# Recurrent gated attention and a mixture of adapters: from chunk-major to batch-major units of 128 tokens and 8 heads

## The chip, the cores and the metric

The kernel runs on one core of a Trainium2 chip. The core has five engines that work side by side and meet through semaphores: TensorE (matrix products, PE in the profile; its weight loads are PEld), VectorE (DVE), ScalarE (ACT), GpSimd (POOL) and SyncE (SP, which here only issues transfers). Data reach the on-chip memory SBUF by DMA; matrix products land in PSUM, eight banks of 2 KB per partition. Each engine takes its own instructions in a fixed order.

The metric is the device time of one execution in microseconds (us), the median of several runs. Differences of under about 0.3% are within what repeated runs of this kernel show.

## The reference, cut to what matters

Shapes: `q, k, v, alpha` are (4 batches, 8 heads, 768 tokens, 48), all float32; the mixture has 8 experts of rank 16 over 384 = 8 x 48 features.

```python
def _attn_ref(q, k, v, alpha):
    state = zeros((B, H, D, D)); y = zeros_like(q)
    for t in range(S):
        state = alpha[:, :, t, :, None] * state + einsum('bhd,bhe->bhde', k[:, :, t], v[:, :, t])
        y[:, :, t] = einsum('bhd,bhde->bhe', q[:, :, t], state)
    return y

def _moe_ref(x, w_gate, A, B):            # x: the 3072 tokens, 384 features (8 heads side by side)
    logits = x @ w_gate                   # the two largest of 8 experts per token
    w = softmax over these two
    delta = sum over the two experts e of  w[e] * ((x @ A[e]) @ B[e])
    return x + delta
```

## The kernel before, in words

The 768 tokens are cut into 6 chunks of 128 (`C`, `NCH`). The main loop (L389) runs over chunks, and one pass handles all 4 batches and 8 heads of that chunk, 32 (batch, head) rows of 48 floats per token.

- `issue_loads` (L156) issues four transfers of 768 KB on SP's queue: `a_t` (alpha, L158), `q_t` (L160), `k_t` (L162), `v_t` (L164). Each moves 32 rows of 192 bytes per partition. The pool `inpool` (L53) has 2 buffers of each, so chunk c+2 waits until chunk c has been read.
- `prologue` (L167), for the next chunk: logarithm of alpha on ACT (`lg`, L173), three products with a triangular matrix (`cum_ps`, L185), two exponentials of each (`acum`, `ainv`, L189 and L190), 32 products with ones for the decay of the chunk (`rs_ps`, L198) and their exponential (`e_rep`, L203), six products of q and k with the exponentials on POOL (`qg` L208, `kg` L210), and the cast of v on DVE (`vb`, L213).
- `state_update` (L292): 32 products of `kg` and `vb` (`kv_ps`, L302), added on DVE to the decayed state (`state`, L307); the decay itself is a product on DVE at the end of the pass (`S_mid`, L404).
- `transposes` (L216): `qg` and `kg` are turned by TensorE (`q_ps` L222, `k_ps` L231) and copied by DVE (`qtq` L227, `ktq` L236).
- `batch_body` (L239), once for each two batches: eight products give the attention of 128 x 128 tokens for 8 heads (`at_ps`, L248), DVE multiplies them with the causal mask (`at_sb`, L253), and TensorE forms `y_ps` from `at_sb` and `vb` (L261) and from `qtq` and the state (L268), one product per head each. ACT copies the result twice, as float32 (`xt`, L274) and as bfloat16 (`xtb`, L281); TensorE turns the latter (`xt_ps`, L288) and DVE copies it (`xT`, L290). `at_ps` and `y_ps` have one buffer each (L62, L63).
- `moe` (L314) works one chunk late, on all four batches at once: logits (`lps`, L320), the two largest on DVE (L325 to L336), an exponential of the difference (L338), weights (L340 to L350), their transposition and spreading over ranks (L353 to L362), the products with A (`zT_ps`, L367), the weighting (`zw`, L372), the products with B (`dl_ps`, L376), the sum with `xt` on DVE (`o_sb`, L378) and the transfer to memory, issued on POOL's queue (L379). The pool `outp` (L60) has 2 buffers.
- `cum_ps`, `rs_ps`, `kv_ps`, `xt_ps`, `lps`, `wT_ps`, `wr_ps`, `zT_ps` and `dl_ps` all share two PSUM buffers (`ps_m`, tag `misc`, L64).

The order of the instructions on each engine is set by the planner of the language, ahead of the run: it takes the program in the order written, but puts an instruction that waits for nothing ahead of one that waits. Semaphores are put in by it too.

## Time and profile before

| | us |
|---|---|
| median of 3 runs (233.31 to 233.94) | 233.45 |
| span of the profiled execution, first to last instruction | 231.6 |
| busy in it: PE | 133.3 |
| DVE | 119.5 |
| ACT | 75.1 |
| POOL | 71.7 |
| transfers of the inputs on SP's queue (share 59.4% of the span) | 137.6 |

The device time is 1.85 us above the profiled span; what lies around the span is taken as that. No engine is busy for more than 58% of the span, and the transfers are finished long before its end. The page gives the sums; where the time goes is read from the order of events, that is from the timeline, the waits and the busy time by stretch, of which the rows stand below.

### The profile page before, as it was taken

The page shows a single profiled execution, that of the slowest core. Times are in us where ns is not written, and L with a number is a line of the kernel's source. Part 1 is how long each engine was busy: PE and PEld are TensorE (multiplying, and loading weights), DVE is VectorE, ACT ScalarE, POOL GpSimd, SP SyncE. Part 2 cuts the span into 40 slices and gives each one's busy share as a digit, 9 for nine tenths or more (in the row PEclk, how much of TensorE's full clock was granted, in tenths as well). Part 3 has the DMA queues.
Part 4 walks back from the last instruction along what each step waited for, and adds up shares of the span by engine and source line. Part 5 has one row for each costly group of instructions (what it writes and reads, how often), then busy time and mean ns, then how long its engine had stood idle before and what let it go on. Part 6 is the DMA issues. An engine that isn't in the chain of part 4 may idle for free.

```text
span 231.6 us, 3686 instructions
## 1 busy us (share of the span) xinstructions
PE 133.3 (58%) x1511; PEld 88.1 (38%) x1512; DVE 119.5 (52%) x230; ACT 75.1 (32%) x132; POOL 71.7 (31%) x88
## 2 busy tenths in 40 slices
PE   0100337888747267468567569458396665696450
PEld 0000225567635026345246336047263354454230
DVE  5300318376953227946508776128956059565531
ACT  2200880831281066051274045750021710221000
POOL 8500490760000288000485001294001590003011
PEclk9999999999999999955555755555555557555555
DMA  7999999999999926994219940300001100002112
GB/s 142 182 160 128 184 186 188 179 191 170 204 176 186 181 72 107 187 189 63 80 59 159 187 65 0 136 3 1 3 0 68 68 3 0 3 0 97 42 47 89
DMA packets 104096, 24.23 MB, mean 105 GB/s; under 512 B 102800, under 2 KB 102928, under 8 KB 104080
## 3 DMA queue, kind: packets, MB, share of 16 engines
q1 hardware_dynamic: 98688, 18.88, 59.4%
q0 software_dynamic: 1536, 4.72, 5.7%
q10 hardware_dynamic: 3856, 0.41, 1.6%
q8 instruction: 12, 0.20, 0.4%
q14 instruction: 4, 0.03, 0.1%
HBM read 19.28 MB, written 4.72 MB: 104 GB/s over the span
## 4 chain that ended last, share of the span: by engine, by line
issue 32%; PE 23%; POOL 13%; ACT 12%; DVE 9%; DMA 9%; POOLq 0%; SPq 0%; DVEq 0%; ACTq 0%
POOL qg L208 6%; POOL kg L210 5%; DMA q_t<-in_q_dram 5%; PE y_ps L261 4%; DMA out_dram<-o_sb 4%; PE y_ps L268 3%; DVE at_sb L253 3%; ACT acum L189 3%; ACT ainv L190 3%; PE k_ps L231 2%; PE zT_ps L367 2%; PE xt_ps L288 2%; PE q_ps L222 2%; POOL out_dram L379 2%; PE kv_ps L302 2%
## 5 line engine op out<-in xcount | busy, mean ns | idle before, releaser
L379 POOL DMA_DIRECT2D out_dram<-o_sb x24 | 14.4, 603 | 125.6 <-DVE o_sb L378 125.0
L261 PE MATMUL y_ps<-vb,at_sb 128*128 128x48 bf16 x192 | 25.2, 218 | 23.9 <-DVE at_sb L253 18.3
L253 DVE TENSOR_TENSOR at_sb<-at_ps,mask 128x1024 bf16<-128x1024 f32 x24 | 29.3, 1219 | 14.1 <-PE at_ps L248 13.9
L274 ACT ACTIVATE xt<-y_ps 128x384 f32<-128x384 f32 x24 | 11.7, 489 | 76.3 <-PE y_ps L268 76.2
L208 POOL TENSOR_TENSOR qg<-q_t,acum 128x528 bf16<-128x528 f32 (+1 forms) x18 | 22.5, 1266 | 30.2 <-ACT acum L189 24.4
L185 PE MATMUL cum_ps<-lg,lsuf 128*128 128x512 bf16 x17 | 9.6, 594 | 37.9 <-ACT ainv L190 21.0
L210 POOL TENSOR_TENSOR kg<-k_t,ainv 128x528 bf16<-128x528 f32 (+1 forms) x18 | 26.8, 1506 | 0.0
L261 PEld LDWEIGHTS <-at_sb 128*128 128x128 bf16 x192 | 13.9, 113 | 33.3 <-DVE at_sb L253 26.5
L227 DVE COPY qtq<-q_ps 128x1024 bf16<-128x1024 bf16 x12 | 8.3, 690 | 28.6 <-PE q_ps L222 28.5
L268 PE MATMUL y_ps<-S_mid,qtq 48*128 48x48 bf16 x192 | 21.3, 218 | 0.0
L378 DVE TENSOR_TENSOR o_sb<-dl_ps,xt 128x384 f32<-128x384 f32 x24 | 12.6, 552 | 13.9 <-DMA out_dram<-o_sb 12.5
L231 PE MATMUL k_ps<-ident_bf,kg 128*128 128x128 bf16 x96 | 15.2, 307 | 7.7 <-POOL kg L210 7.7
L248 PE MATMUL at_ps<-qtq,ktq 48*128 48x128 bf16 x192 | 16.3, 294 | 1.9 <-DVE at_sb L253 1.8
L222 PE MATMUL q_ps<-ident_bf,qg 128*128 128x128 bf16 x96 | 14.8, 310 | 4.1 <-POOL qg L208 2.9
L189 ACT ACTIVATE acum<-cum_ps 128x512 f32<-128x512 f32 x18 | 11.1, 615 | 18.7 <-PE cum_ps L185 18.7
L307 DVE TENSOR_TENSOR state<-kv_ps,S_mid 48x384 bf16<-48x384 f32 x24 | 13.3, 554 | 6.2 <-PE kv_ps L302 5.6
L288 PE MATMUL xt_ps<-ident_bf,xtb 128*128 128x128 bf16 x96 | 14.8, 312 | 2.7 <-DVE o_sb L378 1.4
L198 PEld LDWEIGHTS <-lg 128*48 128x48 bf16 x192 | 5.2, 128 | 28.0 <-ACT ainv L190 17.1
L203 ACT ACTIVATE e_rep<-rs_ps 48x384 f32<-48x384 f32 x24 | 11.7, 486 | 7.3 <-PE rs_ps L198 7.2
L231 PEld LDWEIGHTS <-kg 128*128 128x128 bf16 x96 | 9.4, 137 | 10.4 <-POOL kg L210 9.8
L268 PEld LDWEIGHTS <-qtq 48*128 48x128 bf16 x192 | 10.1, 101 | 6.0
L288 PEld LDWEIGHTS <-xtb 128*128 128x128 bf16 x96 | 10.7, 146 | 4.3 <-issue 2.5
(68 smaller groups left out, 207.5 us busy)
## 6 DMA issues: line engine op xcount, KB each, us to landing
a_t<-in_alpha_dram SPq DMA_DIRECT2D x6, 768.0 KB, 11.0
q_t<-in_q_dram SPq DMA_DIRECT2D x6, 768.0 KB, 10.4
k_t<-in_k_dram SPq DMA_DIRECT2D x6, 768.0 KB, 10.7
v_t<-in_v_dram SPq DMA_DIRECT2D x6, 768.0 KB, 10.9
out_dram<-o_sb POOLq DMA_DIRECT2D x24, 192.0 KB, 2.2
B_st<-in_moe_B_dram ACTq DMA_DIRECT2D x1, 192.0 KB, 3.5
A_st<-in_moe_A_dram ACTq DMA_DIRECT2D x8, 24.0 KB, 5.1
wg_st<-in_moe_w_gate_dram ACTq DMA_DIRECT2D x8, 1.5 KB, 3.5
```

What stands on the lines that cost most here:

```text
L189: nc.scalar.activation(acum_flat[:, t3 * 512:(t3 + 1) * 512], cum_ps, AF.Exp, scale=-1.0)
L208: nc.gpsimd.tensor_tensor(out=qg[:, h0:h1, 0:D], in0=q_t[:, h0:h1, :], in1=acum[:, h0:h1, :], op=ALU.mult)
L210: nc.gpsimd.tensor_tensor(out=kg[:, h0:h1, 0:D], in0=k_t[:, h0:h1, :], in1=ainv[:, h0:h1, :], op=ALU.mult)
L222: nc.tensor.transpose(q_ps[:, j, :], qg[:, 2 * p:2 * p + 2, :].rearrange("a b s -> a (b s)"), ident_bf[:, :],)
L231: nc.tensor.transpose(k_ps[:, j, :], kg[:, 2 * p:2 * p + 2, :].rearrange("a b s -> a (b s)"), ident_bf[:, :],)
L248: nc.tensor.matmul(at_ps[:, slot, :], ktq[rows, jp, :], qtq[rows, jp, :], start=True, stop=True,)
L253: nc.vector.tensor_tensor(out=at_sb, in0=at_ps, in1=mask8, op=ALU.mult)
L261: nc.tensor.matmul(y_ps[:, tt, j * D:(j + 1) * D], at_sb[:, slot, :], vb[:, bh, :], start=True, stop=False,)
L268: nc.tensor.matmul(y_ps[:, tt, j * D:(j + 1) * D], qtq[rows, jp, :], S_mids[c % 2][rows, p, :], start=False, stop=True,)
L288: nc.tensor.transpose(xt_ps[:, m, :], xtb[:, m, :], ident_bf[:, :])
L307: nc.vector.tensor_tensor(out=S_next[rows, half * 8:(half + 1) * 8, :], in0=kv_ps[rows, :, :], in1=S_mids[c % 2][rows, half * 8:(half + 1) ...
L379: nc.gpsimd.dma_start(out=out[t0:t0 + C, :], in_=o_sb)
```

## The change

The loop order is turned round. Work is cut into 24 units (batch b, chunk c), each of 128 tokens and all 8 heads, and each unit runs attention and then the mixture to its end. Loads come by whole batches: four transfers of 1152 KB each (48 rows of 192 bytes per partition), three buffers deep; batches 0 to 2 are issued at the start and batch 3 when batch 0 has been read. Weights are loaded on SP's queue as well, after batch 0. The prologue works on two chunks of one batch at a time (a "duo") and is written ahead of the units of the duo before. The cast of v moves from DVE to POOL. The state of two heads is kept as one 96-wide block of a 128-row tile, whose off-diagonal quarters are zero; it is carried over in PSUM by a product with the identity, and the decay is applied when it is copied out. The mixture's logits and its products with A are one product of 136 columns; the two largest come from one maximum instruction; the product with B is added to `y` in PSUM, so that no sum on DVE remains. Results go out on SP's queue (`nc.sync`), three buffers deep, in place of POOL's. One activation table is loaded at the start for both functions.

```diff
-    inpool = ctx.enter_context(tc.tile_pool(name="inpool", bufs=2))
-    outp = ctx.enter_context(tc.tile_pool(name="outp", bufs=2))
...
+    loads = ctx.enter_context(tc.tile_pool(name="loads", bufs=3))
     scal = ctx.enter_context(tc.tile_pool(name="scal", bufs=2))
-    qkpool = ctx.enter_context(tc.tile_pool(name="qkpool", bufs=1))
-    trsb = ctx.enter_context(tc.tile_pool(name="trsb", bufs=2))
+    vpool = ctx.enter_context(tc.tile_pool(name="vpool", bufs=3))
+    trsb = ctx.enter_context(tc.tile_pool(name="trsb", bufs=3))
...
+    moep = ctx.enter_context(tc.tile_pool(name="moep", bufs=3))
+    outp = ctx.enter_context(tc.tile_pool(name="outp", bufs=3))
...
+    ps_cum = ctx.enter_context(tc.tile_pool(name="ps_cum", bufs=1, space=PS))
+    ps_tr = ctx.enter_context(tc.tile_pool(name="ps_tr", bufs=1, space=PS))
+    ps_at = ctx.enter_context(tc.tile_pool(name="ps_at", bufs=1, space=PS))
+    ps_y = ctx.enter_context(tc.tile_pool(name="ps_y", bufs=2, space=PS))
+    ps_m = ctx.enter_context(tc.tile_pool(name="ps_m", bufs=2, space=PS))
+
+    nc.scalar.preload_act_table_set("natural_log_exp_and_others")
+
+    def load_batch(b):
+        tiles = []
+        for name, src in (("a_t", alpha), ("k_t", k), ("q_t", q), ("v_t", v)):
+            t = loads.tile([P, H * NCH, 48], F4, name=name, tag=name)
+            nc.sync.dma_start(
+                out=t[:, :, 0:D], in_=src[b].rearrange("h (c j) d -> j (h c) d", j=C))
+            tiles.append(t.rearrange("p (h c) d -> p c h d", h=H)[:, :, :, 0:D])
+        return tiles
+
+    batches = [None] * B
+    batches[0] = load_batch(0)
+
+    W_st = consts.tile([P, NF, NW], F4, name="W_st")
+    for i in range(NF):
+        nc.sync.dma_start(
+            out=W_st[:, i, 0:E * R].rearrange("p (e r) -> p e r", e=E),
+            in_=moe_A[:, i * P:(i + 1) * P, :].rearrange("e f r -> f e r"))
+    nc.sync.dma_start(
+        out=W_st[:, :, E * R:NW], in_=moe_w_gate.rearrange("(i f) e -> f i e", f=P))
+    B_st = consts.tile([P, DM], F4, name="B_st")
+    nc.sync.dma_start(out=B_st, in_=moe_B.rearrange("e r f -> (e r) f"))
+    batches[1] = load_batch(1)
+    batches[2] = load_batch(2)
+
...
+    W = consts.tile([P, NF, NW], F2, name="W")
+    nc.vector.tensor_copy(out=W, in_=W_st)
...
+    def prologue(b, g, ring):
+        a_t, k_t, q_t, v_t = batches[b]
+        cs = slice(g * G, (g + 1) * G)
+        lg, qg, kg = lgs[ring], qgs[ring], kgs[ring]
+        nc.scalar.activation(lg[:, :, :, 0:D], a_t[:, cs], AF.Ln)
+        acum = scal.tile([P, G, H, D], F4, name="acum")
+        ainv = scal.tile([P, G, H, D], F4, name="ainv")
+        dec = scal.tile([P, G, NP], F4, name="dec")
+        for c in range(G):
+            cum = ps_cum.tile([P, 512], F4, name="cum")
+            nc.tensor.matmul(cum[:, 0:DM], tri[:, :], lg[:, c, :, 0:D], start=True, stop=True)
+            for p in range(NP):
+                nc.tensor.matmul(
+                    cum[:, DM + p:DM + p + 1],
+                    lg[:, c, 2 * p:2 * p + 2, :].rearrange("a b s -> a (b s)"), ones[:, :],
+                    start=True, stop=True)
+            nc.scalar.activation(
+                ainv[:, c].rearrange("p h d -> p (h d)"), cum[:, 0:DM], AF.Exp, scale=-1.0)
+            nc.scalar.activation(
+                acum[:, c].rearrange("p h d -> p (h d)"), cum[:, 0:DM], AF.Exp)
+            nc.scalar.activation(dec[:, c, :], cum[:, DM:DM + NP], AF.Exp)
+        for c in range(G):
             nc.gpsimd.tensor_tensor(
+                out=kg[:, c, :, 0:D], in0=k_t[:, g * G + c], in1=ainv[:, c], op=ALU.mult)
             nc.gpsimd.tensor_tensor(
+                out=qg[:, c, :, 0:D], in0=q_t[:, g * G + c], in1=acum[:, c], op=ALU.mult)
+        vb = vpool.tile([P, G, H, D], F2, name="vb")
+        nc.gpsimd.tensor_copy(out=vb, in_=v_t[:, cs])
+        return qg, kg, vb, dec
...
+    def unit(b, c, pro):
+        qg, kg, vb, dec = pro
+        ci = c % G
+        tr = ps_tr.tile([P, 2, NP, P], F2, name="tr")
+        for w, src in enumerate((kg, qg)):
+            for p in range(NP):
+                nc.tensor.transpose(
+                    tr[:, w, p, :],
+                    src[:, ci, 2 * p:2 * p + 2, :].rearrange("a b s -> a (b s)"), ident[:, :])
+        kq = trsb.tile([P, 2, NP, P], F2, name="kq")
+        nc.vector.tensor_copy(out=kq, in_=tr)
+
+        if c + 1 < NCH:
+            kv = ps_m.tile([P, NP, 2, D], F4, name="kv", tag="m")
+            if c > 0:
+                nc.tensor.matmul(
+                    kv.rearrange("p a b d -> p (a b d)"), ident[:, :],
+                    sbd[c % 2].rearrange("p a b d -> p (a b d)"),
+                    start=True, stop=False, skip_group_check=True)
+            for p in range(NP):
+                nc.tensor.matmul(
+                    kv[:, p].rearrange("p b d -> p (b d)"),
+                    kg[:, ci, 2 * p:2 * p + 2, :].rearrange("a b s -> a (b s)"),
+                    vb[:, ci, 2 * p:2 * p + 2, :].rearrange("a b s -> a (b s)"),
+                    start=(c == 0 and p == 0), stop=(p == NP - 1), skip_group_check=True)
+            for hh in range(2):
+                rows = slice(HP * hh, HP * hh + HP)
                 nc.vector.tensor_tensor(
+                    out=sbd[(c + 1) % 2][rows, :, hh, :], in0=kv[rows, :, hh, :],
+                    in1=_bc(dec[rows, ci, :], D), op=ALU.mult)
+
+        at = ps_at.tile([P, 2, NP, P], F4, name="at")
+        for p in range(NP):
+            for hh in range(2):
+                rows = slice(HP * hh, HP * hh + D)
+                nc.tensor.matmul(
+                    at[:, hh, p, :], kq[rows, 0, p, :], kq[rows, 1, p, :],
+                    start=True, stop=True)
+        at_sb = atsb.tile([P, 2, NP, P], F2, name="at_sb")
+        nc.vector.tensor_tensor(
+            out=at_sb.rearrange("p a b t -> p (a b) t"),
+            in0=at.rearrange("p a b t -> p (a b) t"), in1=_bc_mid(mask[:, :], (8,)), op=ALU.mult)
+
+        y = ps_y.tile([P, DM], F4, name="y")
+        first = True
+        if c > 0:
+            for p in range(NP):
+                nc.tensor.matmul(
+                    y[:, p * 2 * D:(p + 1) * 2 * D], kq[:, 1, p, :],
+                    sbd[c % 2][:, p].rearrange("p b d -> p (b d)"),
+                    start=first, stop=False, skip_group_check=True)
+                first = False
+        for p in range(NP):
+            for hh in range(2):
+                h = 2 * p + hh
+                nc.tensor.matmul(
+                    y[:, h * D:(h + 1) * D], at_sb[:, hh, p, :], vb[:, ci, h, :],
+                    start=first, stop=False, skip_group_check=True)
+                first = False
+
+        xb = moep.tile([P, DM], F2, name="xb")
+        nc.scalar.copy(xb, y)
+        xt = ps_m.tile([P, NF, P], F2, name="xt", tag="m")
+        for i in range(NF):
+            nc.tensor.transpose(xt[:, i, :], xb[:, i * P:(i + 1) * P], ident[:, :])
+        xs = moep.tile([P, NF, P], F2, name="xs")
+        nc.vector.tensor_copy(out=xs, in_=xt)
+        z = ps_m.tile([P, NW], F4, name="z", tag="m")
+        for i in range(NF):
+            nc.tensor.matmul(z, xs[:, i, :], W[:, i, :], start=(i == 0), stop=(i == NF - 1))
+        lg_ps = z[:, E * R:NW]
+        mx = moep.tile([P, 8], F4, name="mx")
+        nc.vector.max(mx, lg_ps)
+        df = moep.tile([P, E], F4, name="df")
+        nc.vector.tensor_scalar(df, lg_ps, mx[:, 0:1], None, ALU.subtract)
+        ex = moep.tile([P, E], F4, name="ex")
+        nc.scalar.activation(ex, df, AF.Exp)
+        wu = moep.tile([P, E], F4, name="wu")
+        den = moep.tile([P, 1], F4, name="den")
         nc.vector.scalar_tensor_tensor(
+            out=wu, in0=lg_ps, scalar=mx[:, 1:2], in1=ex, op0=ALU.is_ge, op1=ALU.mult,
+            accum_out=den)
+        rd = moep.tile([P, 1], F4, name="rd")
+        nc.vector.reciprocal(out=rd, in_=den)
+        zw = moep.tile([P, E, R], F2, name="zw")
+        nc.vector.scalar_tensor_tensor(
+            out=zw, in0=z[:, 0:E * R].rearrange("p (e r) -> p e r", e=E), scalar=rd[:, 0:1],
+            in1=_bc(wu[:, :], R), op0=ALU.mult, op1=ALU.mult)
+        zt = ps_m.tile([P, P], F2, name="zt", tag="m")
+        nc.tensor.transpose(zt, zw.rearrange("p e r -> p (e r)"), ident[:, :])
+        zs = moep.tile([P, P], F2, name="zs")
+        nc.vector.tensor_copy(out=zs, in_=zt)
+        nc.tensor.matmul(y, zs[:, :], B_all[:, :], start=False, stop=True, skip_group_check=True)
+        o = outp.tile([P, DM], F4, name="o")
+        nc.scalar.copy(o, y)
+        t0 = b * S + c * C
+        nc.sync.dma_start(out=out[t0:t0 + C, :], in_=o)
+
+    duos = [(b, g) for b in range(B) for g in range(NCH // G)]
+    pros = {0: prologue(0, 0, 0)}
+    for n, (b, g) in enumerate(duos):
+        if n + 1 < len(duos):
+            nb, ng = duos[n + 1]
+            if ng == 0 and nb + 2 < B:
+                batches[nb + 2] = load_batch(nb + 2)
+            pros[n + 1] = prologue(nb, ng, (n + 1) % 2)
+        for c in range(g * G, (g + 1) * G):
+            unit(b, c, pros[n])
```

## Rows read from the trace of the kernel before

**Rows 1.** The page, parts 1 and 2: span, busy times, granted clock, transfer engines' share.

```profile
span 231.6 us, 3686 instructions
PE 133.3 (58%) x1511; PEld 88.1 (38%) x1512; DVE 119.5 (52%) x230; ACT 75.1 (32%) x132; POOL 71.7 (31%) x88
...
PEclk9999999999999999955555755555555557555555
DMA  7999999999999926994219940300001100002112
```

**Rows 2.** Busy time by stretch: start:end, length, busy (instructions) by engine, clock, DMA share, GB/s.

```profile
114.30:147.00 32.70, 22.24 (x253) 14.64 (x253) 19.14 (x37) 15.21 (x24) 10.30 (x10) 0.55 0.60 97
...
128.00:144.00 16.00, 10.57 (x123) 6.92 (x119) 11.68 (x25) 5.54 (x10) 0.00 (x0) 0.61 0.65 84
```

**Rows 3.** Waits: engine and line, what it waited for, total, times, longest.

```profile
DVE o_sb L378 <- DMA out_dram<-o_sb: 12.5, 7, 4.0
...
PE cum_ps L185 <- DVE o_sb L378: 7.4, 3, 4.0
```

**Rows 4.** Timeline: start, length, engine, line, operation, tiles; issues of transfers, ACT's first two.

```profile
0.81 0.44 ACTq L118 DMA_DIRECT2D B_st<-in_moe_B_dram  x1
...
7.80 10.65 ACTq L100 DMA_DIRECT2D A_st<-in_moe_A_dram  x8
...
30.34 4.16 SPq L164 DMA_DIRECT2D v_t<-in_v_dram  x1
...
69.39 4.08 SPq L158 DMA_DIRECT2D a_t<-in_alpha_dram  x1
```

**Rows 5.** Page, parts 3 and 6: packets, MB, share per queue; issue to landing.

```profile
q1 hardware_dynamic: 98688, 18.88, 59.4%
...
q10 hardware_dynamic: 3856, 0.41, 1.6%
...
a_t<-in_alpha_dram SPq DMA_DIRECT2D x6, 768.0 KB, 11.0
...
out_dram<-o_sb POOLq DMA_DIRECT2D x24, 192.0 KB, 2.2
```

**Rows 6.** The chain that ended last, in order of time: start, length, what; its first step.

```profile
1.29 10.98 DMA q_t<-in_q_dram
```

**Rows 7.** Groups by line and form: shapes, count; busy, mean ns; idle before them, releaser.

```profile
L253 DVE TENSOR_TENSOR at_sb<-at_ps,mask 128x1024 bf16<-128x1024 f32 x24 | 29.3, 1219 | 14.1 <-PE at_ps L248 13.9
...
L208 POOL TENSOR_TENSOR qg<-q_t,acum 128x528 bf16<-128x528 f32 x12 | 15.5, 1299 | 30.2 <-ACT acum L189 24.4 <-issue 5.8
...
L378 DVE TENSOR_TENSOR o_sb<-dl_ps,xt 128x384 f32<-128x384 f32 x24 | 12.6, 552 | 13.9 <-DMA out_dram<-o_sb 12.5 <-PE dl_ps L376 1.2
L274 ACT ACTIVATE xt<-y_ps 128x384 f32<-128x384 f32 x24 | 11.7, 489 | 76.3 <-PE y_ps L268 76.2
...
L290 DVE COPY xT<-xt_ps 128x512 bf16<-128x512 bf16 x24 | 10.1, 422 | 3.9 <-PE xt_ps L288 3.8
...
L227 DVE COPY qtq<-q_ps 128x1024 bf16<-128x1024 bf16 x12 | 8.3, 690 | 28.6 <-PE q_ps L222 28.5
...
L173 ACT ACT_TABLE_LOAD x6 | 7.7, 1283 | 1.4 <-PEq L422 1.3
...
L325 DVE TENSOR_REDUCE m<-lps 128x4 f32<-128x32 f32 x6 | 1.1, 184 | 0.4 <-PE lps L320 0.4
```

**Rows 8.** Timeline of TensorE: four bursts of matmuls, start, length, count at the end.

```profile
37.11 1.04 PE L222 MATMUL q_ps<-ident_bf,qg 128*128 128x128 bf16 x8 [1.20 <-DVE qtq L227]
...
45.45 0.61 PE L248 MATMUL at_ps<-qtq,ktq 48*128 48x128 bf16 x8
...
72.29 1.89 PE L367 MATMUL zT_ps<-xT,A_arr 128*128 128x128 bf16 x16
...
203.90 1.89 PE L367 MATMUL zT_ps<-xT,A_arr 128*128 128x128 bf16 x16
```

**Rows 9.** Timeline, the last two results issued on POOL's queue.

```profile
226.97 1.19 POOL L379 DMA_DIRECT2D out_dram<-o_sb  x2 [2.05 <-DVE o_sb L378]
```

More of the change, by code (lines that the diff above doesn't have):

```diff
@@ L63 @@
[L63 to L70 removed]
+    moep = ctx.enter_context(tc.tile_pool(name="moep", bufs=3))
+    outp = ctx.enter_context(tc.tile_pool(name="outp", bufs=3))
+    PS = bass.MemoryType.PSUM
@@ new lines @@
+    ones = consts.tile([P, 1], F2, name="ones")
+    nc.gpsimd.memset(ones, 1.0)
+    lgs, qgs, kgs = [], [], []
+    for i in range(2):
+        for lst, nm in ((lgs, "lg"), (qgs, "qg"), (kgs, "kg")):
+            t = consts.tile([P, G, H, HP], F2, name=f"{nm}{i}")
+            nc.gpsimd.memset(t[:, :, :, D:HP], 0.0)
+            lst.append(t)
+    ident = consts.tile([P, P], F2, name="ident")
+    make_identity(nc, ident)
+    mask = consts.tile([P, P], F4, name="mask")
+    nc.gpsimd.memset(mask, 1.0)
@@ L89 @@
-    nc.gpsimd.affine_select(
-        out=Rmat, in_=Rmat, compare_op=ALU.is_ge, fill=0.0, base=(R - 1),
-        pattern=[[-1, E * R]], channel_multiplier=R,
-    )
-    A_st = consts.tile([P, NM, E, R], F4, name="A_st")
-    nc.gpsimd.memset(A_st, 0.0)
-    for m in range(NM):
-        for which in range(2):
-            base = 64 * which
-            h = 2 * m + which
-            nc.scalar.dma_start(
-                out=A_st[base:base + D, m, :, :],
-                in_=moe_A[:, h * D:(h + 1) * D, :].rearrange("e f r -> f e r"),
-            )
@@ L104 @@
-    A_arr = consts.tile([P, NM, E * R], F2, name="A_arr")
-    nc.vector.tensor_copy(out=A_arr, in_=A_st.rearrange("p m e r -> p m (e r)"))
-    wg_st = consts.tile([P, NM, E], F4, name="wg_st")
-    nc.gpsimd.memset(wg_st, 0.0)
-    for m in range(NM):
-        for which in range(2):
-            base = 64 * which
-            h = 2 * m + which
-            nc.scalar.dma_start(out=wg_st[base:base + D, m, :], in_=moe_w_gate[h * D:(h + 1) * D, :])
-    wg_arr = consts.tile([P, NM, E], F2, name="wg_arr")
@@ L115 @@
-    nc.vector.tensor_copy(out=wg_arr, in_=wg_st)
-    B_st = consts.tile([P, DM], F4, name="B_st")
-    nc.scalar.dma_start(out=B_st, in_=moe_B.rearrange("e r f -> (e r) f"))
+        out=mask, in_=mask, compare_op=ALU.is_ge, fill=0.0, base=0,
+        pattern=[[1, P]], channel_multiplier=-1,
+    )
+    sbd = []
+    for i in range(2):
+        t = consts.tile([P, NP, 2, D], F2, name=f"sbd{i}")
+        nc.vector.memset(t, 0.0)
+        sbd.append(t)
+    W = consts.tile([P, NF, NW], F2, name="W")
@@ L119 @@
+    nc.vector.tensor_copy(out=W, in_=W_st)
     B_all = consts.tile([P, DM], F2, name="B_all")
     nc.vector.tensor_copy(out=B_all, in_=B_st)
-    st_tiles = []
-    for i in range(2):
-        st = persist.tile([P, NPAIR, D], F2, name=f"state{i}")
-        nc.vector.memset(st, 0.0)
-        st_tiles.append(st)
-    qg_tiles, kg_tiles = [], []
-    for i in range(2):
-        qg = qkpool.tile([P, BH, 64], F2, name=f"qg{i}")
-        nc.gpsimd.memset(qg[:, :, D:64], 0.0)
-        kg = qkpool.tile([P, BH, 64], F2, name=f"kg{i}")
-        nc.gpsimd.memset(kg[:, :, D:64], 0.0)
-        qg_tiles.append(qg)
-        kg_tiles.append(kg)
@@ L381 @@
-    loads = [None] * NCH
-    loads[0] = issue_loads(0)
-    if NCH > 1:
-        loads[1] = issue_loads(1)
-    vbs = [None] * NCH
-    vbs[0] = prologue(0, loads[0])
-    xt_lists = [None] * NCH
-    for c in range(NCH):
-        xt_list = [None] * B
-        xt_lists[c] = xt_list
-        state_update(c, vbs[c])
-        qtq0, ktq0 = transposes(c, 0)
-        qtq1, ktq1 = transposes(c, 1)
-        if c >= 1:
-            moe(c - 1, xt_lists[c - 1])
-        if c + 1 < NCH:
-            if c + 2 < NCH:
-                loads[c + 2] = issue_loads(c + 2)
-            vbs[c + 1] = prologue(c + 1, loads[c + 1])
-        batch_body(c, 0, qtq0, ktq0, vbs[c], xt_list)
-        batch_body(c, 1, qtq1, ktq1, vbs[c], xt_list)
-        if c + 1 < NCH:
-            nc.vector.tensor_tensor(
-                out=S_mids[(c + 1) % 2], in0=st_tiles[(c + 1) % 2],
-                in1=e_reps[(c + 1) % 2], op=ALU.mult)
```

281 lines of the change are left out of this document (15 added, 266 removed).

## The prediction

> **What bounds the kernel now.** I read the page first. In the 231.6 us of the profiled execution no engine is busy for more than 58%, and the transfer engines are full for the first 19 of 40 slices and then mostly idle [rows 1]. So neither a single engine nor memory bounds the whole; the limits change on the way. Up to about 75 us the loads are the limit: SP issues nine 768 KB loads one behind the other between 30.34 and 69.39 us, 4.34 us each [rows 4], which is 0.181 MB/us. From then on the period of a chunk is the limit. One period, 114.3 to 147.0, lasts 32.7 us for four (batch, chunk) units, 8.2 us a unit, with PE busy for 22.2, DVE 19.1, ACT 15.2 and POOL 10.3 us [rows 2]: each waits for another for a third of the time or more. The waits show where: `cum_ps` of the next chunk stands behind `o_sb`, which shares its two PSUM buffers, and `o_sb` stands for 12.5 us in all behind results that have not landed, with two buffers [rows 3]. Then ACT, POOL and the transposes run one after another, and the copy of `q_ps` on DVE has 28.6 us of idle time before it [rows 7]. In the second half of a period, 128 to 144, four units of attention and of the mixture pass in 16.0 us with DVE busy for 11.68 us, 73% [rows 2]; that is the best mixing this trace shows.
>
> The row of the clock reads 9 for the first 18 slices and mostly 5 after [rows 1], yet the same 16 products of `zT_ps` take 1.89 us at 72.29 and at 203.90 [rows 8]. So I price products by their durations, which are alike on both sides: 16 of 128 columns take 0.85 us more than 8, 0.83 ns a column, which is the level of 1.2 GHz.
>
> **The change, part by part.** I sum each engine's work for one of the 24 units, find a pace, and then look for what holds units up.
>
> DVE. A product or sum that reads PSUM costs 1219 ns for 1024 elements and 552 for 384, so 152 ns plus 1.04 per element; a bfloat16 copy costs 690 for 1024 and 422 for 512, so 154 plus 0.52 per element; a tiny operation 184 [rows 7]. A unit has one copy of 1024 (`kq`, 0.69), two decays of 192 elements in five units of six (2 x 0.35 x 5/6 = 0.59), one mask (1.22), copies of 384 and 128 (0.36 and 0.22), one weighting of 128 (0.29) and four tiny ones (0.74): 4.1 us. The sums `o_sb`, the casts of v and the state's second addition go; 24 units make 98 us where DVE had 119.5 [rows 1].
>
> PE. Columns streamed per unit: 1024 (transposes of `kg`, `qg`), 576 (identity product and `kv`, on average), 320 and 384 (`y`), 384 (`xt`), 408 (`z`), 128, 384 (the product with B) and 384 (`cum`): 3992 x 0.83 ns = 3.3 us. The eight `at` products go in pairs, 0.61 us where eight full ones took 1.04 [rows 8], so 0.4 us, and four one-column products about 0.1: 3.8 us.
>
> ACT. Four passes over 384 elements at 0.489 [rows 7], half a logarithm of 768 and two tiny ones at most as much each: under 3.4 us. Twelve reloads of its table go, of which the row shows six, 7.7 us [rows 7]; the 3.4 us is under the pace found below, so this brings nothing by itself. POOL. Two products of 384 at 1299/528 ns per element are 1.9 us; the cast of v has no row on POOL, and I bound it by nothing and by that price, 0 to 0.94: at most 2.8 us, hidden as the prologue runs a duo ahead.
>
> Pace. DVE at 100% gives 4.1 us a unit, DVE at the 73% of the best stretch 4.1/0.73 = 5.6. There is more to hand over per unit than before (ten changes of engine from `y` to `o`), but `y` has two buffers, `kq` three, `cum` a bank of its own. I take 5.0, somewhat nearer to the row that was measured.
>
> Loads. The bytes and the 192-byte rows stay: q1 had 98,688 packets for 18.88 MB [rows 5], and 16 x 6144 is 98,304. A load of 1152 KB takes 1.5 x 4.34 = 6.5 us. The first two loads landed at 12.27 us [rows 6]; the rest of batch 0, 3.15 MB, takes 17.4 us more: 29.7. The weights, now on the same queue, took 1.6% of the span on their own [rows 5], 3.7 us: 33.4. Eight loads of batches 1 and 2 land by 33.4 + 52.1 = 85.5, batch 3 by 111.5.
>
> Results. This is the step on which the forecast turns. Results move from POOL's queue to SP's. SP's issue of a load lasts as long as the transfer itself, 4.16 and 4.08 us [rows 4], and a load lands 11.0 us after it was begun [rows 5]: SP is held until the queue takes the load, about 11.0 - 4.3 = 6.7 us ahead of landing. Loads 1 and 2 wait for nothing, so the planner sets them ahead of every result; the trace shows it do so, where the load of B, written last, goes out at 0.81 and those of A, which wait for a memset, at 7.80 [rows 4]. So SP is free of batch 2 at 85.5 - 6.7 = 78.8. The load of alpha for batch 3 waits only for logarithms, done long before, and I set it ahead of the first result too: 85.3. The first result then lands at 85.3 + 6.7 + 1.1 (0.2 MB) = 93.1. The other three loads of batch 3 hold SP for another 19.5 us, to 104.8, and I set the next results behind them: 112.6.
>
> Who waits: the copy `o` on ACT has three buffers. With the weights there at 33.4 and about 4 us from `z` to `o`, unit 0 is done at 37.5, units 1 and 2 at 42.5 and 47.5. Unit 3 would be at 52.5 and waits for 93.1, unit 4 for 112.6; behind `o` stand on ACT the copies `xb` and the exponentials of later units, and so PE and DVE. Before, results had POOL's queue to themselves and landed in 2.2 us with loads in flight [rows 5].
>
> The Trainium skill, "DMA: Bandwidth & Descriptors", section "Queues, rings and completion order", speaks against this edit: each issuing engine has one ring on every transfer engine, consumed in order, while different rings take turns. The rows of SP agree, and the time by that rule is the forecast; without it, the first rival.
>
> The sum. Unit 4 at 112.6, unit 5, held in the second `y` buffer, 1.5 us later, 18 more units at 5.0: 204.1. From the last two issues to the end 231.6 - 226.97 = 4.6 [rows 9]: a span of 208.7. The device time lies 1.85 above the span (233.45 - 231.6): **210.5 us**. With a pace of 4.1 it is 194, with 5.6 it is 221.
>
> **The rivals.** First, the results are not held up: SP reaches them between loads, or the loads leave SP early. For it: a queue with room takes a transfer at once, the load of B in 0.44 us at 0.81 [rows 4]. Against it: the nine equal issues. Then 37.5 + 23 x 5.0 + 4.6 + 1.85 = **159 us**, 138 to 173 with the ends of the pace.
>
> Second, slower: the mixture at the end of each unit makes the units go one by one. Each engine keeps its order, so while a unit goes from `y` to `o` (about 5.5 us by the prices above: `y` 0.8, `xb` 0.5, `xt` 0.5, `xs` 0.4, `z` 0.5, the small steps 1.0, `zw` 0.3, `zt` and `zs` 0.5, product 0.5, `o` 0.5), DVE puts the next unit's mask and copy (1.9) in between: 7.4 us a unit, **254 us**. It decides from a pace of (233.45 - 114.1 - 6.45)/18 = 6.3. Against it: before, with one buffer of `y` and of `at`, four units of attention and mixture passed in 16.0 us [rows 2].
>
> Third, TensorE gets the higher clock. The row of the clock has two slices of 7 in its second half, so the upper level is granted now and then [rows 1]. At 2.4 GHz PE's 3.8 us become about 2 and DVE alone sets the pace, 4.1 to 4.6: **194 to 203 us**. The Trainium skill, "TensorE: Matmul & The Clock Gate", section "What's actually happening", says that activity releases the gate; the row shows it fall back each time.
>
> Fourth, the change does not do what its first words say: denser rows would have to shorten the loads, and I give that nothing, since the packets stay 192 bytes. If they did by a third, SP is free 35 us earlier and the time is 175.
>
> **How the numbers follow.** Forecast (results trapped, pace 4.7 to 5.6) 0.58; trapped with a faster pace 0.07; results free 0.18; shorter loads 0.04; one by one 0.13. Faster by over 0.3% is 0.85, within 0.3% (what a measurement of this kernel can tell from no change) 0.02, slower 0.13. The range leaves out most of the one-by-one case and the fast end of the free one: 158 to 226.
>
> **What would show it.** In the profile after: SP's issues of the loads back to back for 6.5 us each and the first issue of `out_dram` after 75 us; a wait of ACT's `o` for `out_dram` of 30 to 60 us in all, before 115 us; PE nearly idle from about 55 to 93; after 115 us a result every 5 us. A first result out before 50 us proves the trap wrong; a result every 6.3 us or more makes the kernel slower; DVE's busy time far from 98 us proves the prices wrong.

## The result, and the profile of the changed kernel

The changed kernel takes 201.53 us (median of four runs, 200.92 to 201.69) where the kernel before took 233.47 beside it: a ratio of 0.8627, with a 95% interval of 0.861 to 0.8644. The forecast was 210.5, with a range of 158 to 226. The sign and the mechanism (results trapped behind loads) came true, but the closeness of 9 us is partly luck: two terms of the sum were wrong by 33 and 26 us, in opposite directions, as the sections below show. A time is the median of all runs of a kernel; in one kernel below (the weights' loads moved) three of four runs fell into a slower state of the chip, its trace among them, and there the fourth run's time stands.

The page of the changed kernel, parts 1 and 2, to be read beside [rows 1]:

```profile
span 199.9 us, 2870 instructions
...
PE 109.8 (55%) x1064; PEld 77.1 (39%) x1064; DVE 98.1 (49%) x284; ACT 59.0 (30%) x157; POOL 59.7 (30%) x77
...
PEclk9999999968555555555555555555855555555555
DMA  5899989799989999899902101110011011101111
```

DVE is busy for 98.1 us, forecast 98, and the transfer engines are again full for half of the span and idle after it. The device time lies 1.6 us above the span.

SP's timeline, the end of the loads (start, length, operation, count), answers to [rows 4]; below it ScalarE's copies `o`, each of which ends one unit:

```profile
61.54 4.74 SPq L77 DMA_DIRECT2D v_t<-in_v_dram  x1
66.38 6.30 SPq L255 DMA_DIRECT2D out_dram<-o  x3
72.89 0.70 SPq L77 DMA_DIRECT2D a_t<-in_alpha_dram  x1
74.55 4.86 SPq L255 DMA_DIRECT2D out_dram<-o  x1
79.63 0.70 SPq L77 DMA_DIRECT2D k_t<-in_k_dram  x1
...
91.08 106.22 SPq L255 DMA_DIRECT2D out_dram<-o  x20
```

```profile
48.73 0.48 ACT L253 COPY o<-y 128x384 f32<-128x384 f32 x1 [1.83 <-PE y L251]
...
74.04 1.01 ACT L253 COPY o<-y 128x384 f32<-128x384 f32 x2 [13.99 <-DMA out_dram<-o]
...
81.41 0.48 ACT L253 COPY o<-y 128x384 f32<-128x384 f32 x1 [2.90 <-PE y L251]
...
130.85 0.48 ACT L253 COPY o<-y 128x384 f32<-128x384 f32 x1 [2.41 <-PE y L251]
...
170.92 0.48 ACT L253 COPY o<-y 128x384 f32<-128x384 f32 x1 [2.47 <-PE y L251]
```

The trap is plain: three results are done by 49 us and leave only at 66.38, straight after the last load of batch 2; units 3 and 4 come together at 74.04, after ScalarE has stood 13.99 us for a result to land. Then two further results come, then a second stall, taken up in the section on more buffers. From unit 12 (130.85) to unit 18 (170.92), the same place in the next batch, six units take 40.07 us, 6.7 us each. That is the steady pace. The last three units, with no prologue left to run beside them, need 4.6 us or less each.

### The profile page after: what moved, and what is told of

It reads as the page before. It is cut to its first block, busy times and chain, and to the rows that moved or that the text cites. A ratio compares the mean times of both kernels' runs of the same rounds, so it can differ in the third digit from the quotient of the medians.

```text
span 199.9 us, 2870 instructions
## 1 busy us (share of the span) xinstructions
PE 109.8 (55%) x1064; PEld 77.1 (39%) x1064; DVE 98.1 (49%) x284; ACT 59.0 (30%) x157; POOL 59.7 (30%) x77
## 5 line engine op out<-in xcount | busy, mean ns | idle before, releaser
L151 POOL TENSOR_TENSOR kg<-k_t,ainv 128x384 bf16<-128x384 f32 x24 | 23.8, 997 | 76.8 <-ACT ainv L145 38.4
L169 DVE COPY kq<-tr 128x1024 bf16<-128x1024 bf16 x24 | 16.5, 687 | 45.2 <-PE tr L165 30.6
L198 DVE TENSOR_TENSOR at_sb<-at,mask 128x1024 bf16<-128x1024 f32 x24 | 29.4, 1224 | 5.0 <-PE at L194 3.0
L194 PE MATMUL at<-kq 48*128 48x128 bf16 x192 | 15.7, 299 | 22.5 <-DVE kq L169 17.8
L153 POOL TENSOR_TENSOR qg<-q_t,acum 128x384 bf16<-128x384 f32 x24 | 23.6, 997 | 4.4 <-ACT acum L147 2.8
L139 PE MATMUL cum<-lg,tri 128*128 128x384 bf16 x24 | 11.8, 490 | 19.6 <-ACT lg L133 9.9
L165 PE MATMUL tr<-ident,kg 128*128 128x128 bf16 x96 | 15.2, 300 | 11.0 <-POOL kg L151 10.2
L156 POOL CAST vb<-v_t 128x768 bf16<-128x768 f32 x12 | 9.8, 827 | 33.7 <-PE y L214 16.4
L194 PEld LDWEIGHTS <-kq 48*128 48x128 bf16 x192 | 8.6, 123 | 28.7 <-DVE kq L169 22.3
L165 PE MATMUL tr<-ident,qg 128*128 128x128 bf16 x96 | 16.3, 303 | 5.4 <-POOL qg L153 5.4
L186 DVE TENSOR_TENSOR sbd<-kv,dec 64x192 bf16<-64x192 f32 x40 | 14.2, 355 | 7.4 <-PE kv L179 5.6
L206 PE MATMUL y<-sbd,kq 128*128 128x96 bf16 x80 | 10.9, 271 | 12.6 <-ACT o L253 12.6
L214 PE MATMUL y<-vb,at_sb 128*128 128x48 bf16 x192 | 14.3, 218 | 0.5 <-ACT o L253 0.5
```

Of the source, the lines that this page charges most:

```text
L139: nc.tensor.matmul(cum[:, 0:DM], tri[:, :], lg[:, c, :, 0:D], start=True, stop=True)
L151: nc.gpsimd.tensor_tensor(out=kg[:, c, :, 0:D], in0=k_t[:, g * G + c], in1=ainv[:, c], op=ALU.mult)
L153: nc.gpsimd.tensor_tensor(out=qg[:, c, :, 0:D], in0=q_t[:, g * G + c], in1=acum[:, c], op=ALU.mult)
L165: nc.tensor.transpose(tr[:, w, p, :], src[:, ci, 2 * p:2 * p + 2, :].rearrange("a b s -> a (b s)"), ident[:, :])
L169: nc.vector.tensor_copy(out=kq, in_=tr)
L186: nc.vector.tensor_tensor(out=sbd[(c + 1) % 2][rows, :, hh, :], in0=kv[rows, :, hh, :], in1=_bc(dec[rows, ci, :], D), op=ALU.mult)
```

## Experiments

Two theories carried the study. First, the results trapped behind loads on SP's queue cost some 20 us. Second, the pace of 6 to 7 us where 5.0 was forecast, with VectorE 60% busy, comes from the planned order and from prologues that wait for buffers. A third question was why loads left SP sooner than forecast. The planner orders each engine's instructions anew when a buffer or a queue changes, so an edit moves more than itself; where the order stayed the same, it is said.

### Results on another queue

```diff
-        nc.sync.dma_start(out=out[t0:t0 + C, :], in_=o)
+        nc.scalar.dma_start(out=out[t0:t0 + C, :], in_=o)
```

> One edit: the 24 result transfers are set by ScalarE's queue instead of SP's, so they no longer stand behind the loads. The order of the instructions on the other engines is planned anew by the planner. Theory (results trapped behind loads): in the changed kernel unit 3's `o` came at 74.0 us, 25.3 us after unit 2's at 48.7, where a pace of 6 us would have given 6; that is 19 us. Units 7 and 8 came 16.3 us after unit 6 instead of 12; that is 4 more. The time falls by 15 to 24 us, to 177 to 187, the 14.0 us wait of ScalarE's `o` on a result's transfer is gone, and results come about every 6 us from 49 us on. Rival (the stretch is held by the loads of the data themselves, not by the results): the time stays within 2 us of 201.5, and `o` of unit 3 still comes after 70 us.

176.57 us, ratio to the kernel before 0.7558 (0.7539 to 0.7577), just under the range that the theory gave. ScalarE's copies `o` of units 2 and 3:

```profile
50.48 0.48 ACT L253 COPY o<-y 128x384 f32<-128x384 f32 x1 [2.19 <-PE y L251]
...
55.37 0.48 ACT L253 COPY o<-y 128x384 f32<-128x384 f32 x1 [0.17 <-PE y L251]
```

Busy time over one steady batch, `o` of unit 12 to `o` of unit 18 (length, then busy time and instructions of PE, PEld, DVE, ACT, POOL, then granted clock, DMA share, GB/s):

```profile
110.19:145.81 35.62, 21.96 (x269) 16.06 (x267) 23.71 (x71) 13.55 (x39) 13.98 (x15) 0.74 0.10 35
```

Unit 3 comes at 55.37 instead of 74.04, 18.7 us earlier, and it waits for TensorE, not for a result. The last `o` is 24.9 us earlier (171.58 against 196.46). So 18.7 of the 25 us are the hold-up of unit 3; the other 6 come later, where this kernel runs six units in 35.6 us instead of 40.1. Its order is new and its granted clock 0.74 there against 0.54 (the row of the changed kernel stands in the section on one batch). The clock alone does not do it: the four runs of the changed kernel had mean granted clocks of 0.62, 0.90, 0.62 and 0.61 and took 201.57, 201.69, 200.92 and 201.5 us. The order or the queue is left, and no run separates these two.

### More buffers for results, on the old queue

```diff
-    outp = ctx.enter_context(tc.tile_pool(name="outp", bufs=3))
+    outp = ctx.enter_context(tc.tile_pool(name="outp", bufs=8))
```

> One edit: 8 buffers for `o` instead of 3; the results still stand behind the loads on SP's queue. Theory (the trap works through ScalarE's wait for a free `o`): units 3 to 7 no longer wait, the first results still land after 70 us, and the time falls by 12 to 24 us, to 177 to 190, about as with results on another queue. Rival (what is late is the queue itself, so that only moving the results helps): within 2 us of 201.5.

184.42 us, ratio 0.7891 (0.7858 to 0.7924). The results still leave SP late (the first at 66.79), but units 3 to 7 are done at 54.1 to 81.0, since nothing on ScalarE waits for them. Only then, with the next units held:

```profile
80.98 0.48 ACT L253 COPY o<-y 128x384 f32<-128x384 f32 x1 [2.41 <-PE y L251]
...
97.37 0.87 ACT L253 COPY o<-y 128x384 f32<-128x384 f32 x2
```

So the trap works as the prediction had it, through ScalarE's wait for a free `o`; a later stall of 16.4 us stays. A stall of the same length stands between units 6 and 7 of the changed kernel (87.92 to 104.21, 16.3 us) and, at 16.3 us again, in the two runs with other loads below, so it does not hang on how long loads take. With three sets of prologue buffers it is 13.7 us (86.88 to 100.62). With two sets it is not there at all when results go on ScalarE's queue or one batch alone is loaded: 7.7 and 7.4 us at the same place. So two sets alone don't make it. The timeline of the changed kernel shows what it consists of:

```profile
87.92 0.48 ACT L253 COPY o<-y 128x384 f32<-128x384 f32 x1 [2.47 <-PE y L251]
...
94.86 0.52 PE L251 MATMUL y<-B_all,zs 128*128 128x384 bf16 x1
...
98.14 0.21 ACT L235 ACTIVATE ex<-df 128x8 f32<-128x8 f32 x1 [5.19 <-DVE df L233]
...
103.84 0.48 ACT L147 ACTIVATE acum<-cum 128x384 f32<-128x384 f32 x1
104.21 0.87 ACT L253 COPY o<-y 128x384 f32<-128x384 f32 x2
```

The last product of unit 7 ends at 95.38, but ScalarE's order has the exponential of unit 8 (98.14) and seven prologue steps (100.98 to 104.32) ahead of its copy `o`. The stall lies in the planned order; why the planner chose it in these programs stays open.

### Rows that are not adjacent

```diff
-        t = loads.tile([P, H * NCH, 48], F4, name=name, tag=name)
+        t = loads.tile([P, H * NCH, 52], F4, name=name, tag=name)
```

> One edit: a row of 48 floats takes 52 places in the SBUF tile of a load, so that rows are not adjacent; bytes, instructions and their order on each engine are those of the changed kernel. Theory (adjacent rows travel as packets of 768 bytes, and that is why a load took 5.1 us of SP's queue instead of the 6.5 forecast): the packets are 192 bytes again, about 98,300 of them, a load holds SP some 6.3 to 6.6 us, v of batch 2 is set by about 78 us instead of 66, the first results go 10 to 13 us later, and the time is 209 to 218. Rival (the rate comes from fewer other transfers at the time, not from the packets): loads take 5.1 us as now and the time stays within 2 us of 201.5.

209.16 us, ratio 0.8951 (0.893 to 0.8972). The order of every engine is that of the changed kernel, so this is the cleanest run. First the queue of SP of the changed kernel, from part 3 of its page (packets, MB, share of 16 engines), then the same row and two issues of this run:

```profile
q1 hardware_dynamic: 31952, 24.00, 51.5%
```

```profile
q1 hardware_dynamic: 31952, 24.00, 56.0%
...
67.29 5.57 SPq L77 DMA_DIRECT2D v_t<-in_v_dram  x1
72.97 7.05 SPq L255 DMA_DIRECT2D out_dram<-o  x3
```

The number of packets is the same (here and below, the time of a packet is the mean over the trace's records of q1's packets of that size): the theory's mechanism fell, adjacent rows are not what makes the packets large. Yet the time rose, because a packet of 768 bytes took 64.5 ns instead of 56.1. Batch 2 left SP 6.6 us later (72.86 against 66.28), unit 3 came 7.5 us later and the whole kernel ended 7.6 us later: the time is in the theory's range, but for another reason. So the length of the loads passes through the trap to the end nearly one for one.

### Six transfers for one tensor

```diff
-            nc.sync.dma_start(
-                out=t[:, :, 0:D], in_=src[b].rearrange("h (c j) d -> j (h c) d", j=C))
+            for c in range(NCH):
+                nc.sync.dma_start(
+                    out=t.rearrange("p (h c) d -> p c h d", h=H)[:, c],
+                    in_=src[b, :, c * C:(c + 1) * C, :].rearrange("h j d -> j h d"))
```

> One edit: a tensor of a batch is loaded by six transfers, one for each chunk of 128 tokens, into the same places of the same tile; a partition's rows of 48 floats in one transfer are then 8, one head apart, not 48 of equal distance. Bytes are the same; the order is planned anew. In the kernel before, whose loads went chunk by chunk, a packet was 192 bytes and took 22.3 ns; in the changed kernel it is 768 bytes and takes 56.1 ns, and with rows not adjacent in SBUF still 768 bytes, at 64.5 ns. Theory (the whole-batch form of the source, rows of equal distance over all chunks, is what puts four rows into a packet): about 98,300 packets of 192 bytes at 20 to 23 ns, a tensor of a batch holds SP 6.2 to 7 us, and the time is 208 to 222. Rival (the packets come from the tile's dense layout or from batch-major order itself): packets stay at 768 bytes and the time is within 5 us of 201.5.

202.24 us, ratio 0.8672 (0.8634 to 0.8711). The queue's row in part 3, and the end of the loads on SP:

```profile
q1 hardware_dynamic: 106960, 24.01, 55.6%
...
67.59 5.43 SPq L78 DMA_DIRECT2D v_t<-in_v_dram  x6
73.51 1.33 SPq L257 DMA_DIRECT2D out_dram<-o  x3
```

Here each theory got half. The packets are 192 bytes again (98,304 of them), so the whole-batch form of the source is what put four rows into one. But they took 15.5 ns each, not the 22.3 of the kernel before. Rows of one transfer lie apart in SBUF here as in the run with 52 places, so these two compare: four packets of 192 bytes, 61.8 ns, against one of 768, 64.5 ns. Between these two runs, which differ in the number of transfers too, the size of the packet is worth nothing. The adjacent rows are worth about a tenth of the time that a load holds SP (5.6 us a tensor here, 5.1 in the changed kernel, means of the long issues of batches 0 to 2). And the end did not follow this time: SP's queue took the first three results in 1.33 us instead of 6.30, so unit 3 came only 3.2 us later than in the changed kernel. The Trainium skill, "DMA: Bandwidth & Descriptors", section "Specifications", wants 512 bytes or more in a transfer for the full rate. The two packets above don't test that, since a row of a load is 192 bytes in both. But packets of 1536 bytes, one row each, took 69.5 ns for the results of the changed kernel and 65.0 ns for the load of B (on ScalarE's queue) in the kernel before, 22 to 24 bytes per ns where the loads of these runs moved 12 to 14: the trace agrees with the page.

### The kernel before, its loads in four parts

```diff
-        nc.sync.dma_start(out=a_t, in_=chunk_view(alpha, c))
+        for b in range(B):
+            nc.sync.dma_start(
+                out=a_t[:, b * H:(b + 1) * H, :], in_=chunk_view(alpha, c)[:, b * H:(b + 1) * H, :])
...
```

> This one edits the kernel before: each of its loads (one tensor, one chunk, 32 rows of 192 bytes to a partition) is set as four transfers of 8 rows, one for each batch, into the same places; bytes and the order on VectorE, ScalarE and GpSimd are the same. In the changed kernel, packets of 192 bytes in transfers of 8 rows took 15.5 ns, against 22.3 ns in the kernel before. Theory (what made the kernel before's packets slow is the long transfer of 32 rows, whatever the packet's size): packets stay at 192 bytes and take 15 to 18 ns, a tensor of a chunk holds SP 3.2 to 3.8 us instead of 4.1, and the time falls to 212 to 229. Rival (it is what ran beside the loads or the tile's place): 21 to 23 ns a packet and a time within 3 us of 233.4.

230.98 us, ratio 0.9892 (0.987 to 0.9913); the queue's row, beside [rows 5]:

```profile
q1 hardware_dynamic: 99840, 18.88, 56.2%
```

A packet took 20.8 ns (22.3 before), a tensor of a chunk still held SP about 4.2 us. The theory fell: shorter transfers alone don't give the 15.5 ns. These transfers have the form of those above (8 rows, one head apart) with the rows adjacent in SBUF, and go slower, so the gain from adjacent rows is shown for the changed kernel's packets of 768 bytes alone. Why the same 192 bytes went faster in the batch-major kernel stays open.

### Three buffers for a prologue

```diff
-    scal = ctx.enter_context(tc.tile_pool(name="scal", bufs=2))
+    scal = ctx.enter_context(tc.tile_pool(name="scal", bufs=3))
...
-    for i in range(2):
+    for i in range(3):
         for lst, nm in ((lgs, "lg"), (qgs, "qg"), (kgs, "kg")):
...
-            pros[n + 1] = prologue(nb, ng, (n + 1) % 2)
+            pros[n + 1] = prologue(nb, ng, (n + 1) % 3)
```

> One edit: three buffers instead of two for what a prologue writes (lg, qg, kg, and acum, ainv, dec); the order is planned anew. Theory (the pace of 6.0 us after 112 us, where VectorE is only 60% busy, is set by prologues that wait for buffers: GpSimd's kg waits 16 us in all for kv of an earlier unit there): the pace falls to 5.0 to 5.5 us and the time to 183 to 194, with the stall of 49 to 74 us as before. Rival (the pace is the unit's own chain through TensorE, VectorE and ScalarE in the planned order): pace 5.8 to 6.2, time within 4 us of 201.5.

189.40 us, ratio 0.8101 (0.8073 to 0.8129). Waits from 112 to 168 us (total, times, longest), first of the changed kernel, then of this run, last of the run with results on ScalarE's queue, which has two sets:

```profile
POOL kg L151 <- PE kv L179: 16.3, 4, 5.7
...
POOL vb L156 <- PE kv L179: 10.9, 2, 5.6
...
PE tr L165 <- POOL kg L151: 5.0, 7, 1.3
```

```profile
POOL vb L156 <- PE kv L179: 4.8, 1, 4.8
...
POOL kg L151 <- PE kv L179: 4.7, 3, 3.7
...
PE tr L165 <- POOL kg L151: 1.9, 1, 1.9
```

```profile
PE tr L165 <- POOL kg L151: 4.4, 4, 1.7
...
POOL kg L151 <- PE kv L179: 1.4, 1, 1.4
```

Six units now take 34.8 us (5.8 each), and the hold-up up to 73.67 is as before. The theory holds in direction and time; the pace missed its 5.0 to 5.5. The order is new as well, and the run with results on ScalarE's queue came to 35.6 us a batch with two sets, though TensorE stood nearly as long for `kg` there. So this run alone does not show how much is the buffers'.

### One batch loaded

```diff
-    batches[1] = load_batch(1)
-    batches[2] = load_batch(2)
+    batches[1] = batches[2] = batches[3] = batches[0]
...
-            if ng == 0 and nb + 2 < B:
-                batches[nb + 2] = load_batch(nb + 2)
```

> Part of the computation is left out: only batch 0 is loaded, and all 24 units work on its tiles, so that 18 of the 24 units wait for no load and no result stands behind one for long. The planned order is new. Theory (the pace of 6.0 us from 112 us on, and the 5.9 us at which the kernel with results on ScalarE's queue ran from 37 to 172 us, is the planned order's and its two buffers', whatever the loads do): the first `o` at 34 to 37 us, then 5.7 to 6.1 us a unit, time 168 to 180. Rival (loads in flight slow the units, or their data comes late): 5.0 us a unit or less, time 150 to 160.

187.73 us, ratio 0.8039 (0.802 to 0.8059): above the range that the theory gave, and far from its rival. Busy time over one steady batch, in the columns given above, first of the changed kernel, then of this run:

```profile
130.85:170.92 40.07, 26.55 (x269) 18.86 (x266) 24.07 (x71) 13.71 (x39) 13.97 (x15) 0.54 0.09 30
```

```profile
116.67:156.87 40.20, 26.89 (x269) 19.08 (x266) 24.05 (x71) 13.71 (x39) 13.97 (x15) 0.50 0.09 30
```

With no load in flight and none to wait for, a batch takes 40.20 us where it took 40.07. The steady pace has nothing to do with the loads. It is also 6.7 us a unit and not the 6.0 that I had read off a stretch that held the fast last units, which is why the run came out above its range.

### Both edits, and the weights' loads moved

> Two edits together: results on ScalarE's queue, and three buffers for what a prologue writes. Alone they gave 176.6 and 189.4 of 201.5 us. Theory (two separate causes, the trap and the pace): the gains nearly add, 25 and 12, less some 3 since with the third buffer the trap is shorter: first `o` at 37 us, a pace of 5.2 to 5.4 us, time 160 to 170. Rival (the same time counted twice, or the loads of batch 3 become the bound): 173 to 178.

The diffs of the first and of the sixth section together: **169.52 us**, ratio 0.7264 (0.7223 to 0.7305), the fastest of all. The gains of 25.0 and 12.1 alone make 32.0 together; the pace, 5.7 us, missed the 5.2 to 5.4 expected. One steady batch:

```profile
106.12:140.07 33.95, 22.29 (x264) 17.08 (x261) 23.97 (x71) 11.25 (x34) 13.01 (x14) 0.72 0.10 36
```

VectorE is at 71% there, against 60% in the changed kernel.

```diff
-        nc.sync.dma_start(
+        nc.scalar.dma_start(
             out=W_st[:, i, 0:E * R].rearrange("p (e r) -> p e r", e=E),
...
```

> The two edits of the kernel before this one, and the loads of W_st and B_st set by ScalarE's queue at the start instead of behind batch 0 on SP's. Theory (loads of a queue go one after the other on SP, 7.8 us of it for the weights, so batches 1 to 3 are set 7 to 8 us earlier; batch 0 itself is shared with the weights and ends about as now): the first `o` comes at 34 to 37 us, the time is 0 to 6 us under the run without this edit. Rival (the weights delay batch 0 by as much as they are off the queue and nothing after depends on a load): no change, within 1 us.

With the weights on ScalarE's queue too, it is 169.87 us, of one run, between the 168.43 and 170.27 us of two runs without this edit: no change seen, as the rival said. SP set batch 1 at 20.04 instead of 26.49 us, and the first `o` came no earlier.

### The order of the instructions

The hand order, in the slot of unit `u` (`n` is `u + 1`, `m` is `u + 2`), drawn together here into two lines without the conditions for the last units, and the switch of each run, with a remark behind it:

```diff
+        m_xt(u); s_kq(m); m_z(u); s_yi(n); s_y(n); m_ex(u); s_kv(m); s_at(m); s_sbd(m)
+        m_zw(u); m_zt(u); s_atsb(m); m_out(u); s_tr_pe(m + 1); pro(u + 5)
...
-    with _tile.TileContext(nc) as tc:
+    with _tile.TileContext(nc, linearize=True) as tc:                    # by hand
+    with _tile.TileContext(nc) as tc:                                    # hand order, planned
+    with _tile.TileContext(nc, schedule_with_timeline_sim=True) as tc:   # other priorities
```

> The changed kernel with its order written out by hand instead of planned: in the slot of unit u each engine gets the MoE steps of u, y of u+1, and the transposes, state and masked product of u+2, with the prologue of u+5; VectorE gets kq and the state update where it would wait for TensorE and ScalarE. Results go by ScalarE's queue, three buffers for what a prologue writes, as in the run with those two edits (169.5 us). Theory (the pace is the planned order's, with VectorE 60% busy at 6.0 us a unit; the floor is VectorE's 4.1): the first `o` at 36 to 40 us, 4.8 to 5.3 us a unit, time 150 to 166. Rival (TensorE at the lower clock or the units' own chain sets the pace): 5.5 us a unit or more, 168 to 180.

573.61 us, ratio 2.457 (2.4523 to 2.4617). This run says nothing of the theory: the switch that kept my order also put all engines' instructions one after the other. The next two let the planner overlap them again.

> The program of the hand-ordered run, but with its order on each engine planned by the planner again: the run before had put the instructions of all engines one after the other (573.6 us, the sum and not an overlap), so it told nothing of the pace. What is left of the hand order is the sequence in which the steps reach the planner: MoE of u, y of u+1, state and masked product of u+2, prologue of u+5. Theory (the pace is the planned order's): 4.8 to 5.3 us a unit, time 152 to 166. Rival (TensorE at the lower clock or the unit's own chain): 5.4 us or more, 167 to 178.

175.04 us, ratio 0.748 (0.745 to 0.7509). A batch takes 32.9 us from unit 12 on (5.5 a unit), a little under the 33.95 of the run above, but a stall of 12.6 us between units 3 and 4 (54.97 to 67.54), where TensorE is given the transposes and scores (`at`) of three later units first, costs more than that. The 4.8 to 5.3 expected did not come; pace and time are the rival's.

> The program of the run with results on ScalarE's queue and three prologue buffers (169.5 us, 5.5 us a unit), instruction for instruction, with SP's order unchanged; only the planner's way of setting priorities is its other one, and so the order on TensorE, VectorE, ScalarE and GpSimd. Theory (order sets the pace): the pace moves by 0.2 us a unit or more, and the time leaves 165 to 174 in one direction or the other. Rival (buffers, TensorE's clock or the unit's own chain set it, whatever the order): 5.3 to 5.7 us a unit, 166 to 173.

187.97 us, ratio 0.8035 (0.8013 to 0.8057): 18.5 us from the same instructions in another order. ScalarE's timeline, and one steady batch:

```profile
39.10 0.48 ACT L253 COPY o<-y 128x384 f32<-128x384 f32 x1 [1.44 <-PE y L251]
...
56.96 0.37 ACTq L255 DMA_DIRECT2D out_dram<-o  x1
57.38 0.48 ACT L220 CAST xb<-y 128x384 bf16<-128x384 f32 x1 [17.60 <-DMA a_t<-in_alpha_dram]
...
127.14:160.91 33.77, 24.79 (x264) 17.89 (x262) 24.77 (x71) 11.40 (x34) 12.01 (x13) 0.60 0.10 36
```

The theory is half right, and not where I looked. The steady pace is 5.6 us a unit, as in the run with the other order (5.7): it didn't move by 0.2. The 18.5 us are nearly all one stall. The first result's transfer stands in ScalarE's order and is set only at 56.96; in this program it counts on a semaphore that it shares with the load of alpha for batch 2, so it waits until that load has landed (56.86), and everything behind it on ScalarE waits too. A result can so be trapped behind a load on another queue.

## Why the prediction came out as it did

**Prices: right for VectorE.** The 98 us forecast are 98.1. TensorE's 3.8 us a unit were too few: 109.8 us busy make 4.6. The forms show `kq` at 687 ns, the mask at 1224, a decay at 355:

```profile
L198 DVE TENSOR_TENSOR at_sb<-at,mask 128x1024 bf16<-128x1024 f32 x24 | 29.4, 1224 | 5.0 <-PE at L194 3.0 <-PE y L214 1.1
...
L169 DVE COPY kq<-tr 128x1024 bf16<-128x1024 bf16 x24 | 16.5, 687 | 45.2 <-PE tr L165 30.6 <-PE y L206 14.6
...
L186 DVE TENSOR_TENSOR sbd<-kv,dec 64x192 bf16<-64x192 f32 x40 | 14.2, 355 | 7.4 <-PE kv L179 5.6 <-issue 1.2
...
L156 POOL CAST vb<-v_t 128x768 bf16<-128x768 f32 x12 | 9.8, 827 | 33.7 <-PE y L214 16.4 <-PE kv L179 10.9 <-issue 5.7
```

The cast of v, bounded from 0 to 0.94 us a unit, costs 0.41.

**First units: right.** Units 0 and 2 at 36.6 and 48.7, forecast 37.5 and 47.5.

**Loads: wrong, 6.5 us forecast, about 5.1 measured.** SP was free of batch 2 at 66.28, not 78.8. I had given the denser rows nothing because the packets would stay at 192 bytes; they became 768. By the runs, with rows of 192 bytes throughout, the packets' size made no difference and adjacent rows in SBUF a tenth of SP's time; the rest of the difference from 6.5 is open. The rival of shorter loads, at 0.04, was too cheap.

**Order on SP: wrong.** I set alpha of batch 3, and then its other three loads, ahead of the results; the planner put three results ahead of alpha and a fourth ahead of k. Units 3 and 4 were free at 74.0 and 74.5, not at 93.1 and 112.6. ScalarE's wait was 14.0 us, not 30 to 60.

**The trap as such: right.** Moving the results alone, or giving them buffers alone, takes the stall of unit 3 away. The rule of the Trainium skill, "DMA: Bandwidth & Descriptors", section "Queues, rings and completion order", on one ring per issuing engine, consumed in order, agrees with the trace: the first result goes out 0.10 us after the last load's issue ends and lands at 74.01, 0.50 us after that load.

**Pace: wrong, 5.0 forecast.** From unit 5 at 81.41 to the end of unit 23 at 196.94 it is 115.5 us for 18 units, 6.4 each, where I had 90; the stall of 16.3 us after unit 6 is in it. I priced VectorE at 73% to 100% from the best stretch of the kernel before; here it is at 60%. The step I left out, as far as the runs show it, is that the prologue of the next duo has only two sets of buffers, so GpSimd's `kg` stands for `kv` of an earlier unit, and TensorE's transposes, which its order has ahead of mixture products, stand for `kg` (seven times from 112 to 168 us, 5.0 us). A third set, with the order planned for it, brings 34.8 instead of 40.1 us a batch. Buffers and order are not taken apart by it: with results on ScalarE's queue, two sets in another order gave 35.6 us, with `kg` standing 1.4 us for `kv` instead of 16.3 and TensorE 4.4 us for `kg` instead of 5.0, and there the third set brought only 1.7 us more (33.95). The loads have no part in it (40.20 us without them). Between 34 us a batch and VectorE's 4.1 us a unit lies more: three orders with three sets and results on ScalarE's queue all gave 5.5 to 5.7 a unit, and what bounds these is not settled. Granted clocks of 0.50 (the lower level, 1.2 GHz, throughout) and 0.54 gave the same 40 us, and 0.60 and 0.72 the same 34, and the run of the changed kernel at 0.90 (most of the span at the upper level, 2.4 GHz) was no faster than those at 0.62. So it isn't the clock, and the prediction's third rival, a gain from the higher clock, falls with that run.

**How the errors cancel.** Unit 5 came 32.7 us earlier than in the sum (81.4 against 114.1), the 18 units after it took 25.5 us longer, and the tail (3.0 for 4.6 us) and the time outside the span (1.6 for 1.85) took 1.8 less: 210.5 - 32.7 + 25.5 - 1.8 = 201.5. The point at which the one-by-one rival turns slower, 6.3 us, moved with unit 5: from 81.4 it is (233.45 - 81.4 - 6.45)/18 = 8.1, so a steady pace of 6.7 was harmless.

## What to carry to other kernels

Before results go onto the queue that carries the loads, write that queue's order down to the last prefetch: the buffers of the result then decide how long every engine behind it stands, and a queue of its own, or only more buffers, gave back 17 to 25 us here. A pace read from an engine's best stretch is a hope: list the buffers that the next stage's first instruction writes, and who read them last. And read a steady pace from one place in a batch to the same place in the next, not from a stretch that holds the end.
